# Two of the last four output blocks begun in side banks, the last 128 features in strips of their own, stores shared by two queues, and a new instruction order in an attention kernel on one core

## The chip, the cores and the metric

The kernel runs on one core of a Trainium2 chip. The metric is the device time of one execution in microseconds. The core has five engines, each with an instruction stream of its own that is executed in order: TensorE (PE in the profile, with its weight loads as PEld), VectorE (DVE), ScalarE (ACT), GpSimd (POOL) and SyncE (SP, which here only issues DMAs). Engines wait for each other with semaphores. Matmuls write to PSUM, which has eight banks of 128 partitions by 512 float32 values; everything else lies in SBUF or, for copies that change the layout, in DRAM scratch tensors.

## The reference

Two attention layers read their own inputs' weights but the same activations x (2048 tokens, 640 features, 32 heads of 20), and a gate mixes their outputs:

```python
x = A_x
g = _sigmoid((x * gate_w).sum(-1, keepdims=True))
a = _A_ref(x, A_wqkv, A_wo)      # full softmax attention: scores of 2048 x 2048 for each of 32 heads
b = _B_ref(x, B_wqkv, B_wo)      # each token looks at 8 tokens, at distances 0, 2, ... 14 behind it
return g * a + (1 - g) * b
```

In `_A_ref`, `scores = q k^T * Dh ** -0.5`, `p = softmax(scores)`, `o = p v`, and `o @ wo`. `_B_ref` does the same over the 8 gathered keys. The output is 2048 x 640 in bfloat16. Nearly all of the work is the exponential of 32 x 2048 x 2048 scores.

## The kernel before, in words

**Groups and tiles.** The 2048 queries are taken in four chunks of 512 (`qc`), the 32 heads in eight sets of four (`q`). A pair (qc, q) is a group, 32 in all, in the order of `GROUPS`. A group has 64 units: 16 blocks of 128 keys times 4 heads. One unit is a score matmul of 32 rows (20 features, a bound that keeps the exponent in range, and zeros) by 512 queries; four heads lie in four row strips of the array and run side by side. `next_tile` (line 1890) forms a score tile of two or three units, `qk` (1942; the matmuls are line 1955) writes it to one of two PSUM tensors, `score0` and `score1`, and `exp` (1970; line 1973) turns it into `ebuf` on ScalarE, 1024 or 1536 columns at a time. `pv` (1982; line 2018) multiplies `ebuf` by the values into `obank`, two tiles later. `vA` holds a column of ones, so that the denominators come out with the sums.

**Rides.** ScalarE can't take all units. A fourth kind of unit "rides" with a tile of two: its scores go to the third bank of the tile's PSUM tensor, and VectorE makes a coarse exponential of it by rounding to the bits of a bfloat16 (`clamp`, line 1932, into `uD`); three shifted copies (`gen_d`, line 1048, or on POOL `piece`, line 1079, into `eD`) with weighted values (`gen_vs`, line 1098) correct it, so such a unit needs four PV matmuls instead of one. `wanted` (1813) decides whether a tile takes a ride, `lone` (2052) sends one by itself.

**Banks.** PSUM holds `score0` and `score1` (three banks each), `obank` and `side0`. All other matmuls (projections, local attention, output blocks) borrow one of three side banks: bank 0 is `side0`, banks 1 and 2 are the third banks of `score0` and `score1`, and `bank()` (655) hands out whichever is free first. So a third unit, a ride and a side matmul compete for the banks 1 and 2.

**Who sets the order.** The order of every engine is computed while the program is built. `_Sched.task` (263) appends an instruction to its engine's list and keeps an estimate of when it ends; side work is written as Python generators (`gen_...`) with priorities, which `run_side` and `spend` step forward while the estimate shows room before the next score tile. Twenty-two knobs of that (slacks, due times, thresholds, how many products POOL takes, when a filler matmul is put in to keep TensorE busy, line 2039) come from the table `PLAN` (52), which has an entry for every fifth or tenth tile. Changing one entry changes the order of everything behind it.

**Side work.** `gen_q1`, `gen_qd`, `gen_kd` and `gen_v` project queries, keys and values; `gen_bproj` and `gen_b` do the local attention in eight pieces of 256 tokens (`u`): products on VectorE (line 1216) and POOL, sums over features by TensorE (1229), an exponential `eT` on ScalarE (1261), a trip through DRAM (`scr_e`, then `eB`) that spreads it over partitions (`gen_relay`, 1177), products with the values (1325) and sums (1337). `gen_norm` (972) normalises a finished group and moves it by DMA to `oTd`, and `gen_fold` (1488) forms the output rows of the first three chunks, 128 rows at a time, from `oB` (local) and `oTd` (full).

**The end.** The last four output blocks (the 512 queries of the last chunk) can't wait for `gen_fold`. `gen_prefold` (1386) sums, for their columns 0 to 511 of blocks 0 and 1 and for the last 128 columns of all four, what is ready early, and parks it in SBUF (`pre`). `gen_prefold2` (1425) sums columns 0 to 511 of the blocks 2 and 3 in a side bank each and leaves them there (`tail_bank`). It begins when the normalised heads of all groups but the last are there and no more rides are to come (`d_over`). `tail` (1436) then adds on TensorE (line 1447) what came late: two feature chunks for the last 128 columns of all four blocks, which lie side by side in one bank of `score1` (the strips), the same two chunks for columns 0 to 511 of blocks 0 and 1 in two banks of `score0` (the halves), and finally the last group's heads (`oN`, from `gen_norm_last`, 936) for strips, side banks and halves. VectorE adds strips (1471) and halves (1480) to what was parked, ScalarE copies the blocks 2 and 3 out (1477), and four DMAs of 128 rows store them (1485): blocks 2 and 3 from ScalarE's queue, 0 and 1 from SP's.

## Time and profile before

| what | us |
|---|---|
| median of 3 runs (778.37 to 778.88) | 778.65 |
| profiled execution, its own time | 778.55 |
| span from its first to its last instruction | 776.7 |
| ScalarE busy, of which line 1973 | 756.5, 742.9 |
| TensorE busy | 749.7 |
| VectorE busy | 697.6 |
| POOL busy | 359.0 |
| mean of one exponential of 1024 columns (513 of them) | 1.076 |
| mean of one exponential of 1536 columns (196 of them) | 1.520 |

The profile gives one execution. A line of it names an engine, the line of the kernel, the operation, the tile written and the tiles read, the count, and then the busy time with the mean of one, and the idle time of the engine before it with what ended that idle time. Consecutive instructions of an engine overlap a little, so a mean is longer than the step from one to the next. The timeline gives start and length in us from the start of the span, with equal neighbours merged (the form shown is the first one's). A granted clock of 9 in the page's row of tenths means the full TensorE clock.

### The profile page before, as it was taken

The numbers are of one execution on the slowest core, as the hardware profiler recorded it, in microseconds if no ns is written. First come the engines' busy times: TensorE is split into PE (matmuls) and PEld (weight loads), VectorE is DVE, ScalarE is ACT, GpSimd is POOL, SyncE is SP. The second block draws the span as 40 slices with busy tenths as digits, with TensorE's granted clock in tenths as the row PEclk, the third lists the DMA queues.
The fourth block names the chain that finished last, engine by engine and source line by source line (L and its number), as shares of the span: only waits on it lengthen the run. The fifth ranks groups of instructions, "written<-read, shape, count | busy, mean of one in ns | idle before, by whom it ended". The sixth has DMA issues, their size and how long they took to land.

```text
span 776.7 us, 30340 instructions
## 1 busy us (share of the span) xinstructions
PE 749.7 (97%) x12484; PEld 290.9 (37%) x12484; DVE 697.6 (90%) x1270; ACT 756.5 (97%) x751; POOL 359.0 (46%) x616
## 2 busy tenths in 40 slices
PE   9999999999999999999999999999999999999997
PEld 6433333232334333334344334433444433343232
DVE  6798989999899999979899989999999998899895
ACT  6999999999999999999999999999999999999995
POOL 4345744455453542545355445434545433344441
PEclk9999999999999999999999999999999999999999
DMA  7421221021121435201124112323124133102301
GB/s 231 117 60 39 48 66 40 21 47 35 34 72 47 100 79 115 61 26 37 38 64 110 32 48 67 96 66 92 45 51 106 34 78 96 52 19 63 88 12 36
DMA packets 71457, 49.91 MB, mean 64 GB/s; under 512 B 43096, under 2 KB 64872, under 8 KB 71320
## 3 DMA queue, kind: packets, MB, share of 16 engines
q1 hardware_dynamic: 70376, 47.54, 24.4%
q8 instruction: 100, 1.64, 0.9%
q10 hardware_dynamic: 944, 0.43, 0.2%
q14 instruction: 37, 0.30, 0.1%
HBM read 32.79 MB, written 7.62 MB: 52 GB/s over the span
## 4 chain that ended last, share of the span: by engine, by line
PE 49%; ACT 30%; issue 13%; DVE 6%; DMA 1%; SPq 0%; ACTq 0%; DVEq 0%
ACT ebuf L1973 30%; PE score L1955 16%; PE obank L2018 14%; PE side L681 12%; PE score L681 4%; DVE uD L1932 2%; DVE eD L1048 1%; DMA oB<-in_A_x_dram 1%; PE side L1337 1%; PE side L1229 1%; PE score L2039 1%; DVE kvw L1216 0%; PE score L1666 0%; PE obank L2039 0%; DVE dst L831 0%
## 5 line engine op out<-in xcount | busy, mean ns | idle before, releaser
L1973 ACT ACTIVATE ebuf<-score 128x1024 bf16<-128x1024 f32 (+1 forms) x710 | 742.9, 1198 | 5.1 <-PE score L1955 3.6
L1932 DVE TENSOR_SCALAR uD<-score 128x512 int16<-128x512 f32 x433 | 291.3, 684 | 33.8 <-PE score L1955 31.6
L1955 PE MATMUL score<-qT,kT 32*128 32x512 bf16 x1856 | 258.8, 384 | 12.6 <-ACT ebuf L1973 9.3
L1079 POOL TENSOR_TENSOR eD<-uD,two 128x256 int32<-128x256 int32 x331 | 198.2, 613 | 136.0 <-DVE eD L1048 61.6
L1048 DVE TENSOR_SCALAR eD<-uD 128x2048 int16<-128x2048 int16 (+3 forms) x302 | 173.2, 596 | 3.1 <-PE obank L2018 2.3
L2018 PE MATMUL obank<-ebuf,vA 128*21 128x512 bf16 x1615 | 152.8, 385 | 1.3 <-ACT ebuf L1973 1.1
L1955 PEld LDWEIGHTS score<-qT,kT 32*128 32x128 bf16 x1856 | 63.8, 91 | 209.0 <-ACT ebuf L1973 148.1
L1098 POOL TENSOR_TENSOR vS<-vA,vw 128x252 bf16<-128x252 bf16 x109 | 67.2, 617 | 110.3 <-DVE eD L1048 64.5
L2018 PE MATMUL obank<-eD,vS 128*21 128x512 bf16 x1299 | 113.1, 379 | 0.0
L681 PE MATMUL side<-xT,wBs 128*32 128x256 bf16 x2400 | 97.7, 282 | 1.7 <-DVE qkvB L1154 0.8
L681 PEld LDWEIGHTS side<-xT,wBs 128*32 128x32 bf16 x2400 | 67.4, 142 | 34.1 <-issue 16.8
L1021 POOL TENSOR_TENSOR oN<-oTt,oN 128x256 bf16<-128x256 f32 x60 | 45.2, 754 | 50.8 <-DVE eD L1048 27.8
L2018 PEld LDWEIGHTS obank<-ebuf,vA 128*21 128x21 bf16 x1615 | 37.0, 89 | 82.9 <-issue 56.7
L1325 DVE TENSOR_TENSOR kvw<-kvw,eB 128x2048 bf16<-128x2048 bf16 (+1 forms) x40 | 45.8, 1171 | 0.0
L1154 DVE CAST qkvB<-side 128x512 bf16<-128x512 f32 (+1 forms) x72 | 42.1, 594 | 2.5 <-PE side L681 2.4
L1216 DVE TENSOR_TENSOR kvw<-qkvB 128x2048 bf16<-128x2048 bf16 (+2 forms) x40 | 43.6, 1124 | 0.1
L2018 PE MATMUL obank<-uD,vA 128*21 128x512 bf16 x433 | 42.3, 379 | 0.0
L2018 PEld LDWEIGHTS obank<-eD,vS 128*21 128x21 bf16 x1299 | 31.8, 91 | 20.0 <-issue 2.5
L1006 POOL TENSOR_TENSOR rcp<-rcp,gA 128x16 f32<-128x16 f32 x30 | 7.4, 248 | 58.1 <-DVE eD L1048 33.2
L1955 PE MATMUL score<-woBp,kT 32*128 32x512 bf16 x192 | 29.5, 384 | 1.8 <-ACT ebuf L1973 1.8
L681 PE MATMUL side<-xT,kvw 128*32 128x512 bf16 (+1 forms) x360 | 29.8, 382 | 0.3 <-DVE vA L907 0.2
L1207 POOL TENSOR_TENSOR kvw<-qkvB 128x256 bf16<-128x256 bf16 x29 | 17.5, 614 | 26.9 <-DVE kvw L1216 11.4
(201 smaller groups left out, 578.9 us busy)
## 6 DMA issues: line engine op xcount, KB each, us to landing
kvw<-scr_v SPq DMA_DIRECT2D x32, 336.5 KB
oN<-scr_n SPq DMA_DIRECT2D x60, 128.0 KB
scr_v<-qkvB SPq DMA_DIRECT2D x32, 85.0 KB
wBs<-in_B_wqkv_dram SPq DMA_DIRECT2D x5, 480.0 KB
WqP<-in_A_wqkv_dram SPq DMA_DIRECT2D x14, 160.0 KB
oTd<-oN SPq DMA_DIRECT2D x108, 20.0 KB
out_dram<-outsb SPq DMA_DIRECT2D x12, 160.0 KB
qT<-dst SPq DMA_DIRECT2D x93, 20.0 KB
```

Source lines behind the costliest of these rows:

```text
L681: ins = e.matmul(o[j:k, :], l(j) if callable(l) else l[:, j:k], r, start=(first and i == 0), stop=(last and i == n - 1), skip_group_check= ...
L1021: T("pool", 0.73, lambda e, cols=cols: e.tensor_tensor(oN[0][:, cols], oTt[:, cols], rcpR[:, cols], ALU.mult), reads=["oTt", "oN%d" % i], ...
L1048: T("dve", 0.065 + 0.1334 * (n - m), lambda e, k=k, sl=sl, m=m: e.tensor_scalar(eD[:, sl % NS, 512 * m:512 * n].bitcast(I16), uD[d % 2][:, ...
L1079: T("pool", PDUR, lambda e: e.tensor_tensor(eD[:, sl % NS, 512 * i:512 * (i + 1)].bitcast(I32), uD[d % 2][:, 512 * i:512 * (i + 1)].bitcas ...
L1098: T("pool", 0.607, lambda e: e.tensor_tensor(vS[:, d % 2, :, :], _ap(vA, (kb * NQ + q) * 4 * DV, [[0, K - 1], [1, 4 * DV]]), _ap(vw, 0, [[ ...
L1154: t = TB(dvc(n * TOK), lambda e, o=o, i=i: e.tensor_copy(o, i), reads=[("side", b)], writes=[key])
L1216: TB(dvc(n_ * TOK, 2), lambda e: e.tensor_tensor(o, i0, i1, ALU.mult), reads=["qB", "kB"], writes=prods(i, range(n_)) + olds(), port=True)
L1325: TB(dvc(n_ * 2 * TOK, 2), lambda e: e.tensor_tensor(o, i0, i1, ALU.mult), reads=rd, writes=prods(i, range(2 * n_)), port=True)
L1932: t = T("dve", 0.598, lambda e: e.tensor_scalar(uD[d % 2][:, 512 * i:512 * (i + 1)].bitcast(I16), side[x], UOFF, 0.0, op0=ALU.add, op1=ALU ...
L1955: ins = e.matmul(o, kT[32 * j:32 * j + 32, q, kb * P:(kb + 1) * P], qT[qbuf[g]][32 * j:32 * j + 32, :], start=True, stop=True)
L1973: exps[s] = T("act", actc(512 * n), lambda e: e.activation(ebuf[s % NE][:, 0:512 * n], score[s % 2][:, 0:512 * n], ACTF.Exp, scale=LN2 / S ...
L2018: ins = e.matmul(obank[32 * j:32 * j + DV, :], v, src, start=(kb == 0), stop=(last and k >= len(lst) - 4), skip_group_check=True)
```

## The change

It has five parts. They are told here in the order in which they act.

1. `PLAN` has other values from the first tile on and 128 entries instead of 121, so the instruction order differs on every engine from about the tenth tile to the end. The computation is the same.
2. Rides in another bank: where the knob `FRT` is 0 or more (ten of the table's entries), a tile that carries a ride may take a third unit too, and the ride's scores go to bank 0 or to the other tile's third bank (`rbank`).
3. Two of the last blocks in side banks: `gen_prefold2` asks for bank 0 for block 2 and bank 1 for block 3, begins block 2 when the last group has begun, with the local part and the first three feature chunks, and takes the other two chunks when the heads of all groups but the last are there. While 14 units or fewer of the last group are left, tiles leave bank 1 free (`TLAST` in `crowded`).
4. The last 128 columns: the strips of the blocks 2 and 3 lie in one bank of `score1` and those of 0 and 1 in the next, each pair with a key of its own, and VectorE adds each pair by itself; the halves have keys of their own as well. `gen_norm_last` turns the first half of the heads back before it scales the second, and the last group's matmuls run in the order block 2, strips 2 and 3, block 3, strips 0 and 1, half 0, half 1.
5. Stores: blocks 2 and 0 go by SP's queue, 3 and 1 by ScalarE's; the planner's estimate of a store has a case of its own (`svc < 0`), which changes no instruction by itself.

```diff
 PLAN = {
-    0: ((0.326, 0.478), 0.0, 1, 1.0, 0.79, -1.09, -0.25, 10.72, 2.0, 9.17, 0.45, 0.36, 3.46, 3.61, 0.0, 0.59, 1, -2.32, 0.3, -1.0, (2, 2), 0.2),
+    0: ((0.326, 0.478), 0.0, 1, 1.0, 0.79, -1.09, -0.25, 5.46, 2.0, 9.17, 0.45, 0.36, 3.46, 3.61, 0.0, 0.59, 1, -2.32, 0.3, -1.0, (2, 2), 0.2),
...
-        for op, h in ((turn_o, 1), (turn_o, 0), (inv, 1), (inv, 0), (gate_r, 1), (gate_r, 0), (scale_o, 1), (scale_o, 0), (back, 1), (back, 0)):
+        for op, h in ((turn_o, 1), (turn_o, 0), (inv, 1), (inv, 0), (gate_r, 1), (gate_r, 0), (scale_o, 1), (back, 1), (scale_o, 0), (back, 0)):
             op(h)
...
     def gen_prefold2():
-        while not (done.get("prefold1") and d_over() and all(done.get(("norm", POS[QCN - 1, q])) for q in range(1, NQ)) and done.get("wz")):
-            yield ("cond",)
-        rd = [("oTd", (QCN - 1) % 2, q) for q in range(NQ)] + ["woA_d"] + WOB + WQ + oBk(QCN - 1, range(2))
+        early = sorted({h // 4 for f in range(FE) for h, o, r, m in pieces[f]})
+        while not (done.get("prefold1") and cur["g"] >= NG - 1 and done.get("wz")):
+            yield ("cond",)
+        rd = [("oTd", (QCN - 1) % 2, q) for q in early] + ["woA_d"] + WOB + oBk(QCN - 1, range(2))
         qs = None
         for blk in (2, 3):
-            b = yield from bank()
-            yield from mm_group(b, fold_mms(side[b][:, :], blk, qs, 0, 512, True), rd, mmc(512), last=False)
+            while blk > 2 and not d_over():
+                yield ("cond",)
+            b = yield from bank(blk - 2)
+            yield from mm_group(b, fold_mms(side[b][:, :], blk, qs, 0, 512, True, range(FE)), rd, mmc(512), last=False)
+            while not all(done.get(("norm", POS[QCN - 1, q])) for q in range(1, NQ)):
+                yield ("cond",)
+            yield from mm_group(b, fold_mms(side[b][:, :], blk, qs, 0, 512, True, range(FE, CN)),
+                                [("oTd", (QCN - 1) % 2, q) for q in range(NQ)] + WQ, mmc(512), first=False, last=False)
             tail_bank[blk] = b
...
-        strip = lambda blk: b3[:, blk * P:(blk + 1) * P]
+        sof = lambda blk: 512 * (blk < 2) + blk % 2 * P
+        strip = lambda blk: b3[:, sof(blk):sof(blk) + P]
...
-        mm(("score", 1), [m_ for blk in range(4) for m_ in first(strip(blk), blk, q, 512, D)], False, rl)
-        mm(("score", 0), [m_ for blk in range(2) for m_ in first(half(blk), blk, q, 0, 512)], False, rl)
+        for h in (1, 0):
+            mm(("strip", h), [m_ for blk in (2 * h, 2 * h + 1) for m_ in first(strip(blk), blk, q, 512, D)], False, rl, [("score", 1)][:h])
+        for blk in range(2):
+            mm(("half", blk), first(half(blk), blk, q, 0, 512), False, rl, [("score", 0)][blk:])
         run_until(("norm", NG - 1))
+        for h, blk in ((1, 2), (1, None), (1, 3), (0, None), (0, 0), (0, 1)):
+            if blk is None:
+                mm(("strip", h), [fold_mms(strip(i), i, q, 512, D, False)[0] for i in (2 * h, 2 * h + 1)], True, rd[h])
+            elif h:
+                mm(("side", tail_bank[blk]), fold_mms(side[tail_bank[blk]][:, :], blk, q, 0, 512, False), True, rd[h])
+            else:
+                mm(("half", blk), fold_mms(half(blk), blk, q, 0, 512, False), True, rd[h])
         for h in (1, 0):
-            mm(("score", 1), [fold_mms(strip(blk), blk, q, 512, D, False)[0] for blk in (2 * h, 2 * h + 1)], True, rd[h])
...
-        T("dve", dvc(512), lambda e: e.tensor_tensor(
-            _ap(stage, 3 * 1024 + 512, [[D, 4], [1, P]]), _ap(b3, 0, [[P, 4], [1, P]]),
+            T("dve", dvc(256), lambda e, h=h: e.tensor_tensor(
+                _ap(stage, 3 * 1024 + 512 + 2 * h * D, [[D, 2], [1, P]]), _ap(b3, sof(2 * h), [[P, 2], [1, P]]),
...
-            T("act" if blk > 1 else "sp", 2.0, lambda e, blk=blk, row=row: e.dma_start(out_v[row:row + P, :], tout[blk]),
-              reads=[("tout", blk), "tout_r"], writes=[("out", row)], dma=True, iss=0.45)
+            T("act" if blk % 2 else "sp", 2.0, lambda e, blk=blk, row=row: e.dma_start(out_v[row:row + P, :], tout[blk]),
+              reads=[("tout", blk), ("tout_r", blk // 2)], writes=[("out", row)], dma=True, iss=0.45, svc=-0.6)
...
                 if ride:
-                    break
+                    alt = [b for b in ((0, 3 - x) if FRT >= 0.5 else (0,) if FRT >= 0 else ()) if not bank_used[b] and bank_free[b] <= now + 0.05]
+                    if not alt or sum(bank_used) == NB - 1 or lo == 4 * ahead[g][1]:
+                        alt = None
+                        break
...
+    TLAST = 14
+
     def crowded(x):
...
-        return sum(bank_used) == 1 and any(ent[3][0] == "bank" and ent[0] <= xprio() for ent in gens) and bank_free[x] <= min(
+        return cur["g"] == NG - 1 and x == 1 and 4 * ahead[NG - 1][1] - ahead[NG - 1][0] <= TLAST and "prefold" not in done or sum(bank_used) == 1 and any(ent[3][0] == "bank" and ent[0] <= xprio() for ent in gens) and bank_free[x] <= min(
             [bank_free[b] for b in range(NB) if not bank_used[b]])
...
-                    add_gen(gen_prefold2(), 2.3)
+                    add_gen(gen_prefold2(), 0.9)
```

More of the change, by code (lines that the diff above doesn't have):

```diff
@@ L309, in task @@
             t.end = start + dur
-            if stream == "sp" and start > 35.0:
+            if svc < 0:
+                self.ring = max(self.ring, start + 0.55) - svc
+                t.end = self.ring + 1.0
+            elif stream == "sp" and start > 35.0:
                 fin = max(max(self.ring, start + 1.4) + svc, start + 1.4 + iss * (nd - 1) + svc / nd)
@@ L653, in _build, with bank @@
     xheld = [None]
-    def bank():
+    def bank(*only):
         while True:
-            got = yield ("bank",)
+            got = yield ("bank", *only)
             if got is not None:
@@ L1450, in mm @@
             T("pe", sum(0.215 if o.shape[-1] > 128 else 0.06 for o, _, _ in lst), fn, reads=rd, mode="col",
-              **({"accum": [key]} if accum else {"writes": [key]}))
+              **({"accum": [key]} if accum else {"writes": [key] + list(old)}))
         b3 = score[1]
@@ L1795, in _build @@
     rides = []
+    rbank = []
     UNIT = 0.46
@@ L1964, in qk @@
         t = T("pe", 0.2155 * max(js.count(j) for j in js), fn, reads=sorted(rd, key=str),
-              writes=[("score", s % 2)] + ([("side", x)] if len(lst) == 3 else []), mode="row")
+              writes=[("score", s % 2)] + ([("side", x)] if len(lst) >= 3 else []) + ([("side", rbank[s])] if rides[s] and rbank[s] != x else []),
+              mode="row")
         if rides[s]:
-            clamp(t, d, i, x)
+            clamp(t, d, i, rbank[s])
     def exp(s):
```

23 lines of the change are left out of this document (9 added, 14 removed), and 241 rows, old and new, of the table PLAN.

## The prediction

> **What bounds the kernel now.** I read the page first (busy time by engine, then its costliest groups), then ScalarE's part of the timeline, then the timeline of the last 12 us, then the chain that ended last.
>
> ```profile
> PE 749.7 (97%) x12484; PEld 290.9 (37%) x12484; DVE 697.6 (90%) x1270; ACT 756.5 (97%) x751; POOL 359.0 (46%) x616
> ...
> PEclk9999999999999999999999999999999999999999
> ...
> L1973 ACT ACTIVATE ebuf<-score 128x1024 bf16<-128x1024 f32 (+1 forms) x710 | 742.9, 1198 | 5.1 <-PE score L1955 3.6
> ```
>
> ScalarE spends 742.9 us of a span of 776.7 in one line, the exponentials of the score tiles. By form these are 513 of 1024 columns, 196 of 1536 and one of 512. Its timeline gives the pace at which they follow each other when nothing holds them:
>
> ```profile
> 16.30 0.47 ACT L1693 ACTIVATE kT<-obank,onesrow 128x256 bf16<-128x256 f32 x1
> 17.29 33.27 ACT L1973 ACTIVATE ebuf<-score 128x1536 bf16<-128x1536 f32 x31 [0.53 <-PE score L1955]
> ...
> 50.77 6.50 ACT L1973 ACTIVATE ebuf<-score 128x1024 bf16<-128x1024 f32 x7
> ...
> 253.62 1.08 ACT L1973 ACTIVATE ebuf<-score 128x1024 bf16<-128x1024 f32 x1
> ...
> 580.53 2.92 ACT L1973 ACTIVATE ebuf<-score 128x1536 bf16<-128x1536 f32 x2
> ...
> 583.19 2.95 ACT L1973 ACTIVATE ebuf<-score 128x1536 bf16<-128x1536 f32 x2
> ...
> 765.85 1.69 ACT L1973 ACTIVATE ebuf<-score 128x1024 bf16<-128x1024 f32 x2
> ```
>
> Seven of 1024 columns take 6.50 us and one lasts 1.08, so the step is (6.50-1.08)/6 = 0.904 us. Two of 1536 lie between 580.53 and 583.19: 1.33 us a step. The exponentials start at 17.29 and the last ends at 765.85+1.69 = 767.54, 750.25 us later. At the free pace they need 513x0.904 + 196x1.331 + 0.73 = 725.4; the 21 other ScalarE instructions in between add about 5.6 (0.47, 0.11 and 0.14 from their neighbours' starts). So 19.2 us are lost because a score tile came late, in pieces of mostly under half a microsecond that the page's 5.1 us of idle shows only in part. From the starts of all tiles, stretches of 50 tiles lose between 1.1 and 2.6 us, 1.8 in the mean (the other instructions, 0.4, included).
>
> The remaining 9.15 us (767.54 to 776.7) are the end:
>
> ```profile
> 767.59 0.61 PE L2018 MATMUL obank<-ebuf,vA 128*21 128x512 bf16 x8 [0.28 <-ACT ebuf L1973]
> 768.03 0.82 PE L681 MATMUL score<-woBp,oB 128*32 128x512 bf16 x12
> ...
> 768.26 0.78 DVE L940 STREAM_TRANSPOSE oTt<-obank 128x256 f32<-128x256 f32 x2 [3.43 <-PE obank L2018]
> ...
> 769.39 0.78 DVE L955 TENSOR_TENSOR oN<-oTt,rcp 128x256 bf16<-128x256 f32 x2
> ...
> 770.06 0.50 DVE L959 STREAM_TRANSPOSE oN<-oN 128x128 f32<-128x128 f32 x2
> ...
> 770.85 0.39 PE L1447 MATMUL score<-WqP,oTd 128*32 128x512 bf16 x4
> 771.07 0.28 PE L1447 MATMUL score<-outsb,oN 128*32 128x128 bf16 x8
> ...
> 771.95 0.69 DVE L1471 TENSOR_TENSOR kvw<-score,kvw 128x512 bf16<-128x512 f32 x1 [1.39 <-PE score L1447]
> ...
> 773.15 0.68 DVE L1480 TENSOR_TENSOR kvw<-score,qabs 128x512 bf16<-128x512 f32 x1
> ...
> 773.26 0.94 SPq L1485 DMA_DIRECT2D out_dram<-kvw  x2
> ```
>
> The reader is to see that the normalised heads oN stand ready at 770.56, but TensorE comes to them only at 771.07: it is still clearing output-block work that stands ahead in its queue. The chain of work that ended last says the same:
>
> ```profile
> 767.59 0.61 PE obank L2018 x8
> 768.20 1.73 PE score L681 x32
> 769.93 1.42 PE score L1447 x56
> ...
> 771.95 0.69 DVE kvw L1471
> 772.64 0.60 DVEq L357
> ```
>
> **The sum's base.** The profiled execution took 778.55 us, of which 776.70 are the span; the median of the runs is 778.65, 0.10 above it. A measurement of this kernel can tell about 0.2% (1.56 us) from no change.
>
> **Head: 0.** The list of head operations is untouched; the first tile still leaves at 17.29.
>
> **Exponentials: +0.2.** Counted in the built program, the new order has 500 of 1024, 205 of 1536 and one of 512 (1616 units of 512 columns instead of 1615, one clamp on VectorE fewer): 452.0 + 272.9 + 0.7 = 725.6 against 725.4. ScalarE remains the bound. The Trainium skill, in "ScalarE: Activation LUTs" under "Rules for kernel authors", budgets about 0.3 us for each ACTIVATE plus 0.83 ns an element; by that, 13 short ones fewer and 9 long ones more would be an estimated -0.8, and the sum 1.0 lower than mine. The trace disagrees: the fixed part in 0.904 us for 1024 columns is about 0.05 us.
>
> **Tiles that come late: -1.4.** The planner's table is new for nearly every stretch, so every stretch between the first ten tiles and the end is ordered anew. What does not change: PV, projection and local-attention matmuls differ by three instructions; VectorE's shifted copies become fewer and longer (178 of 2048 columns for 169, 19 of 512 for 36), with row means of 704 and 297 ns and the other forms -0.4 us in all; POOL makes 20 copies fewer (0.61 us each, on an engine busy 46%). SP's queue holds as many transfers of each kind as before (60 reads of oN, 16 eB loads and so on), in another order. Two things ease TensorE, whose lateness is the loss. There are 706 score tiles instead of 710, and a tile costs 0.32 us (753.86 to 754.18 in the timeline) and about 0.10 of switching beside its neighbours: 4x0.42 = -1.7. And of the places where a PV matmul waits for VectorE, POOL or ScalarE there are 309 instead of 351; the page's waits put 10.8, 6.6 and 1.3 us on such places, and 12% of these 18.7 is -2.2. The 72 missing filler matmuls (304 for 376, 18 groups of four at 0.215 us = 3.9 us) count for nothing, since they stand where TensorE had nothing to do. TensorE's 3.9 us only help where it was late. Bounds: -3.9 and 0. But some 38 tiles of 710 carry 10.8 of the 19.2, and which of them are touched is not to be seen, so I stay nearer to 0 and take -1.4. A new order is also a new draw: the 14 stretches scatter by 0.43 us, which is 1.6 over all, so 8 times in 10 within 2.1 either way. The rides in another bank change little by themselves: 4 of 432 go to the spare bank.
>
> **End: -0.9.** Removed from behind the last PV matmul: 16 of the 32 matmuls of block 3 (4 groups, 0.86 us), which now stand ahead of it. Ahead there is room: before, 8 matmuls ran from 766.70 to 767.13 and TensorE then waited until 767.59, so 8 more (0.43) end as the last exponential does, and the other 8 stand one and two tiles earlier. TensorE's backlog then ends at 771.07-0.86 = 770.2. VectorE becomes the bound there: the first half's back transpose follows its own scaling, at about 769.9 instead of 770.06, ready at 770.2; the second half's is pushed behind scaling two and comes 0.3 later, at 770.9. First-half matmuls (0.54 us) run from about 770.35, second-half ones (0.54) from 771.0, and TensorE ends at 771.7 instead of 772.3. The strip addition becomes two of 256 columns, 0.42 each (the row of 256-column L955 is 0.44) and 0.34 apart, the first from 771.0 beside the matmuls. The two 0.60 steps of L1480 then end at 773.0 against 773.83. This adds one instruction, 0.1 us against one of 512. Stores: SP's second issue at 773.86 landed by 775.91; now ScalarE issues blocks 3 and 1, SP 2 and 0, the last at 773.0; ScalarE has nothing else left, and its issues took 0.35 and 0.45 us and landed 1.84 and 1.93 us later. Gain between 0.6 (TensorE's end alone) and 1.2 (0.86 and the second issue's 0.34); I take 0.9, by the additions' ends. One wait moves closer: block 2's last 8 matmuls need the oTd moves of the last group but one, and the last two score tiles stand behind them. The transpose ahead of the moves stands about 16 us before the last exponential's end, the moves need 3.69 to issue and some 1.9 to land, the use comes 2.5 before the end: 8 us of cover, so 0. The bank kept free during the last 14 units changes forms only, and is in the count above.
>
> **Sum.** 778.55 + 0.2 - 1.4 - 0.9 = 776.45, rounded 776.5.
>
> **Rivals.**
> *Only the end gains:* the new order loses as the old (19.2), as the near-equal tally of TensorE's work per pair of tiles suggests (326 pairs over ScalarE's pace before, 318 after). 777.9, inside 0.2%.
> *The new order is much better:* every stretch loses what the better half of them did before, 1.4 instead of 1.8: 14x0.35 = -4.9, and 773.0. For it speaks only that TensorE's order is lighter in 8 of 14 stretches.
> *The new order loses more:* in tiles 300 to 350, 450 to 500 and 600 to 650 TensorE's work exceeds ScalarE's by 1.2, 0.1 and 0.3 us, where it stayed 0.5, 1.0 and 0.2 below. TensorE is in order, so each excess is ScalarE's idle time. Five of 14 stretches at the worst row (2.6 us for 1.8) make +3.9 where I have -1.4: 781.8. It decides from 3.7 us above my sum on. Against it: over all tiles that work is 5.9 us lighter.
> *The last local-attention piece is late:* its exponential eT now stands 12 tiles ahead of the first matmul that sums its products, where 23 tiles lay between (5x1.33 + 8x0.904 + 0.6 = 14.5 us to the next need). Issue, two DMA trips and product take 0.84+1.80+1.9+1.18+1.9+1.2+0.6 = 9.4 by the rows, so 5 us of cover. Were 19.8 us needed from eT to the first product as before (713.95 to 733.74), TensorE would stand for 7: 783.5. Against it: VectorE did not wait for that product, the old order merely put it there.
> *The clock:* the granted clock is 1.00 everywhere except 0.97 in the last 9.1 us, where TensorE empties. If each of the 18 missing filler groups left such a dip (0.27 us), this costs 4.9: 781.4. The Trainium skill, "TensorE: Matmul & The Clock Gate", Part 1, says that an idle window of some 3.4 us halves the clock. Against it: the emptiest 25 us still have TensorE busy for 23.1.
>
> **How the numbers follow.** Forecast 0.54 (0.50 of it beyond 0.2%), much better 0.10, only the end 0.22, loses more 0.08, late piece 0.04, clock 0.02. Faster 0.60, same 0.26, slower 0.14. Range 774.0 to 779.4: it leaves out the second case for the most part and the three slow ones; the likeliest case alone spans 774.4 to 778.6 (2.1 either way).
>
> **What would show it.** ScalarE's last exponential should end near 766.3 with 706 instructions and a busy time within 2 us of 742.9. Behind it the oN matmuls of block 2 should begin about 770.35-767.54 = 2.8 us after it (3.5 before), the last L1480 successor should end 5.4 us after it (6.3), the span 8.2 (9.15). The step on which I trust least is the lateness: should the exponentials end at 767.5 or later, it failed; should VectorE's second back transpose or a store come later than said, the end did.

## The result and the profile after

The changed kernel takes 776.25 us (median of 6, 775.56 to 776.46), the kernel before in the same series 778.72 (778.37 to 779.77): a ratio of 0.9965, 95% interval 0.9953 to 0.9978. The forecast was 776.5. From the page of the changed kernel, busy times and the line of the exponentials:

```profile
PE 743.5 (96%) x12409; PEld 291.0 (38%) x12409; DVE 696.8 (90%) x1263; ACT 756.6 (98%) x747; POOL 353.8 (46%) x603
...
PEclk9999999999999999999999999999999999999999
...
L2000 ACT ACTIVATE ebuf<-score 128x1024 bf16<-128x1024 f32 (+1 forms) x706 | 743.2, 1198 | 3.0 <-PE score L1981 1.6
```

Line numbers have moved: the exponentials stand in line 2000 (1973 before), score matmuls in 1981, PV in 2045, fillers in 2066, side matmuls in 691, the tail's in 1464, strip additions in 1490, half additions in 1499, stores in 1504. By the rows of the two traces the orders first differ at 58.5 us, at the 40th tile (not from about the tenth, as the section on the change has it). ScalarE is the bound as before: 706 exponentials, 743.2 us for 742.9. Its timeline has the start of the first and the end of the last:

```profile
18.00 27.84 ACT L2000 ACTIVATE ebuf<-score 128x1536 bf16<-128x1536 f32 x26 [0.53 <-PE score L1981]
...
765.80 0.60 ACT L2000 ACTIVATE ebuf<-score 128x512 bf16<-128x512 f32 x1
```

With the prediction's pace (0.904 and 1.331 us a step) the span of one profiled execution falls into four terms. "Loss" is the time from the first exponential's start to the last one's end, less that pace; the other ScalarE instructions (about 5.6) are in it for both kernels.

| term, us | before | after | difference | predicted |
|---|---|---|---|---|
| first exponential begins | 17.29 | 18.00 | +0.71 | 0 |
| exponentials at their own pace | 725.36 | 725.59 | +0.23 | +0.2 |
| loss | 24.89 | 22.82 | -2.07 | -1.4 |
| behind the last exponential | 9.21 | 8.02 | -1.19 | -0.9 |
| span | 776.75 | 774.43 | -2.32 | -2.1 |

The timeline of the end, all engines:

```profile
766.47 0.61 PE L2045 MATMUL obank<-ebuf,vA 128*21 128x512 bf16 x8
766.90 0.82 PE L691 MATMUL score<-woA_d,oTd 128*32 128x512 bf16 x12
767.13 0.78 DVE L950 STREAM_TRANSPOSE oTt<-obank 128x256 f32<-128x256 f32 x2 [6.78 <-PE obank L2045]
...
768.75 0.31 DVE L969 STREAM_TRANSPOSE oN<-oN 128x128 f32<-128x128 f32 x1
...
769.12 0.10 PEld L1464 LDWEIGHTS side<-outsb,oN 128*32 128x32 bf16 x4 [0.37 <-DVE oN L969]
769.12 0.40 PE L1464 MATMUL side<-outsb,oN 128*32 128x512 bf16 x4
769.34 1.18 PE L1464 MATMUL score<-outsb,oN 128*32 128x128 bf16 x28
769.43 0.31 DVE L969 STREAM_TRANSPOSE oN<-oN 128x128 f32<-128x128 f32 x1
...
769.68 0.89 DVE L1490 TENSOR_TENSOR kvw<-score,kvw 128x256 bf16<-128x256 f32 x2
769.80 0.23 PEld L1464 LDWEIGHTS score<-outsb,oN 128*32 128x32 bf16 x16 [0.29 <-DVE oN L969]
...
770.19 1.37 SPq L1504 DMA_DIRECT2D out_dram<-kvw  x2
770.49 0.68 DVE L1499 TENSOR_TENSOR kvw<-score,dst 128x512 bf16<-128x512 f32 x1
770.68 1.45 ACTq L1504 DMA_DIRECT2D out_dram<-kvw  x2
771.08 0.68 DVE L1499 TENSOR_TENSOR kvw<-score,qabs 128x512 bf16<-128x512 f32 x1
```

The last exponential ends at 766.40. The matmuls of the last heads begin at 769.12, 2.7 us later (2.8 forecast, 3.5 before), as soon as the first half of the heads stands ready (769.06); the last addition ends at 771.76, 5.35 us later (5.4 forecast, 6.3 before). TensorE's weight loads (PEld) now wait for VectorE's back transposes, 0.37 us for the first half of the heads and 0.29 for the second, where the kernel before had the heads ready 0.5 us before TensorE came to them. So VectorE sets the pace there, as the prediction said. The chain that ended last shows this only in part, since TensorE still has matmuls to run up to that point:

```profile
767.07 0.86 PE score L691 x16
767.94 1.31 PE score L1464 x48
769.25 0.27 PE side L1464 x4
769.52 0.60 PE score L1464 x20
...
770.57 0.60 DVE kvw L1499
```

### The profile page after: what moved, and what is told of

Read it like the earlier page. It is cut to its first block, busy times and chain, and to the rows that moved or that the text cites. A ratio compares the mean times of both kernels' runs of the same rounds, so it can differ in the third digit from the quotient of the medians.

```text
span 774.4 us, 30166 instructions
## 1 busy us (share of the span) xinstructions
PE 743.5 (96%) x12409; PEld 291.0 (38%) x12409; DVE 696.8 (90%) x1263; ACT 756.6 (98%) x747; POOL 353.8 (46%) x603
## 4 chain that ended last, share of the span: by engine, by line
PE 45%; ACT 33%; issue 15%; DVE 6%; DMA 1%; SPq 0%; ACTq 0%; DVEq 0%
ACT ebuf L2000 33%; PE score L1981 14%; PE obank L2045 13%; PE side L691 11%; PE score L691 4%; DVE uD L1958 2%; DVE eD L1058 1%; DMA oB<-in_A_x_dram 1%; PE side L1239 1%; PE score L2066 0%; PE score L1685 0%; PE side L1347 0%; PE obank L2066 0%; DVE dst L841 0%; DVE kvw L1226 0%
## 5 line engine op out<-in xcount | busy, mean ns | idle before, releaser
L2000 ACT ACTIVATE ebuf<-score 128x1024 bf16<-128x1024 f32 (+1 forms) x706 | 743.2, 1198 | 3.0 <-PE score L1981 1.6
L1958 DVE TENSOR_SCALAR uD<-score 128x512 int16<-128x512 f32 x428 | 286.0, 681 | 30.0 <-PE score L1981 28.0
L1089 POOL TENSOR_TENSOR eD<-uD,two 128x256 int32<-128x256 int32 x311 | 186.7, 615 | 123.3 <-DVE eD L1058 59.3
L1108 POOL TENSOR_TENSOR vS<-vA,vw 128x252 bf16<-128x252 bf16 x108 | 65.4, 606 | 111.7 <-DVE eD L1058 66.0
L2045 PE MATMUL obank<-eD,vS 128*21 128x512 bf16 x1296 | 110.7, 379 | 0.0
L691 PE MATMUL side<-xT,wBs 128*32 128x256 bf16 x2400 | 95.6, 281 | 0.7 <-DVE rQ L1301 0.5
L1031 POOL TENSOR_TENSOR oN<-oTt,oN 128x256 bf16<-128x256 f32 x60 | 47.5, 791 | 58.7 <-DVE eD L1058 29.3
L1226 DVE TENSOR_TENSOR kvw<-qkvB 128x1792 bf16<-128x1792 bf16 (+2 forms) x40 | 44.4, 1133 | 0.1
L691 PE MATMUL side<-kvw,xT 128*32 128x160 bf16 (+1 forms) x760 | 28.5, 262 | 0.5
```

The lines of the kernel that those rows point to most:

```text
L691: ins = e.matmul(o[j:k, :], l(j) if callable(l) else l[:, j:k], r, start=(first and i == 0), stop=(last and i == n - 1), skip_group_check= ...
L1031: T("pool", 0.73, lambda e, cols=cols: e.tensor_tensor(oN[0][:, cols], oTt[:, cols], rcpR[:, cols], ALU.mult), reads=["oTt", "oN%d" % i], ...
L1089: T("pool", PDUR, lambda e: e.tensor_tensor(eD[:, sl % NS, 512 * i:512 * (i + 1)].bitcast(I32), uD[d % 2][:, 512 * i:512 * (i + 1)].bitcas ...
L1108: T("pool", 0.607, lambda e: e.tensor_tensor(vS[:, d % 2, :, :], _ap(vA, (kb * NQ + q) * 4 * DV, [[0, K - 1], [1, 4 * DV]]), _ap(vw, 0, [[ ...
L1226: TB(dvc(n_ * TOK, 2), lambda e: e.tensor_tensor(o, i0, i1, ALU.mult), reads=["qB", "kB"], writes=prods(i, range(n_)) + olds(), port=True)
L1958: t = T("dve", 0.598, lambda e: e.tensor_scalar(uD[d % 2][:, 512 * i:512 * (i + 1)].bitcast(I16), side[x], UOFF, 0.0, op0=ALU.add, op1=ALU ...
```

## The experiments

Each kernel ran beside the kernel before on one chip. The table gives medians, the kernel before in the same series, the ratio's 95% interval, and from one profiled execution the terms of the table above; "additions" is the end of the last addition, counted from the end of the last exponential.

| kernel | median | before | ratio | first | loss | additions | span - last exponential |
|---|---|---|---|---|---|---|---|
| before | 778.72 | | | 17.29 | 24.89 | 6.29 | 9.21 |
| changed | 776.25 | 778.72 | 0.9953-0.9978 | 18.00 | 22.82 | 5.35 | 8.02 |
| old table | 776.68 | 778.81 | 0.9966-0.9983 | 18.27 | 25.53 | 5.35 | 7.67 |
| old end | 778.00 | 778.81 | 0.9982-0.9999 | 17.07 | 22.64 | 6.51 | 9.80 |
| small fillers | 776.80 | 778.81 | 0.9971-0.9988 | 17.93 | 23.80 | 5.35 | 8.14 |
| score matmuls doubled | 789.48 | 778.81 | 1.0120-1.0156 | 18.10 | 37.55 | 5.35 | 7.99 |
| old back order | 776.61 | 778.86 | 0.9956-0.9980 | 17.49 | 22.98 | 5.40 | 8.40 |
| old queues | 776.68 | 778.86 | 0.9956-0.9981 | 17.25 | 22.64 | 5.35 | 8.19 |
| PV cut | 777.01 | 778.86 | 0.9966-0.9984 | 17.50 | 21.87 | 5.34 | 8.21 |
| entry 400 nudged | 798.18 | 778.86 | 1.0229-1.0257 | 17.92 | 36.78 | 13.76 | 16.07 |
| PV doubled | 785.65 | 778.66 | 1.0075-1.0106 | 17.49 | 32.25 | 5.35 | 8.05 |
| eleven local nudges | 776.11 | 778.66 | 0.9955-0.9978 | 17.80 | 22.70 | 5.35 | 7.97 |
| old table, entry 485 nudged | 803.91 | 778.66 | 1.0308-1.0336 | 17.73 | 31.17 | 24.56 | 27.34 |
| one strip addition | 776.96 | 778.35 | 0.9971-0.9990 | 17.84 | 22.85 | 5.63 | 8.63 |

Two columns say how to read the rest. Kernels with the same order lose the same: the changed kernel, old back order, old queues, eleven nudges and one addition lie between 22.64 and 22.98, and the additions end at 5.35 wherever the end's code is the same. What scatters from execution to execution is the start, 17.07 to 18.27 in instructions that no kernel changed, and the landing of the last stores. The profiled execution need not be a typical one: those of "PV cut" and "old queues" are the shortest of their kernels (774.97 and 775.48 us).

**The table and the end, each alone.** The old table in the changed code, and the old end in the changed order:

```diff
-PLAN = { (128 entries) }
+PLAN = { (the 121 entries of the kernel before) }
```

> The changed kernel with the old table: the instruction order is that of the kernel before on every engine up to TensorE's 12159th of 12458 matmuls, and only the end is new. Theory (the parts add up, the order of the stretches brought most of it): the exponentials lose what they lost before, 24.9 us with the other ScalarE instructions, and end near 767.4 (17.3 + 725.1 + 24.9), the end behind them takes 8.0 to 8.2 instead of 9.2, so 777.4 to 777.7, 1.0 to 1.2 below the kernel before. Rival (the end's gain hangs on the new order, TensorE's queue being emptier there): the end takes 9.0 or more and the time is 778.4 or more. Second rival (the end brings all of it): 776.5 or less.

```diff
-    def gen_prefold2(): ... block 2 in bank 0, block 3 in bank 1, begun early
-    def tail(): ... strips by pairs, stores in turn
-    def gen_norm_last(g): ... scale 1, back 1, scale 0, back 0
+    (the three functions of the kernel before)
...
-    add_gen(gen_prefold2(), 0.9)
+    add_gen(gen_prefold2(), 2.3)
...
-        return cur["g"] == NG - 1 and x == 1 and 4 * ahead[NG - 1][1] - ahead[NG - 1][0] <= TLAST and "prefold" not in done or sum(...
+        return sum(...
```

> The changed kernel with the old end: the new table and the rides in another bank, but blocks 2 and 3 begun late, one strip bank, old order of the last matmuls and old stores; the order is that of the changed kernel up to TensorE's 12215th of 12411 matmuls. Theory (the parts add up): exponentials 497 x 0.904 + 207 x 1.331 + 0.7 = 725.5, loss as in the changed kernel 22.8, ended near 766.4, the end behind them 9.2 as before: 777.3 to 777.7, 1.0 to 1.4 above the changed kernel. Rival (the changed kernel's smaller loss was a matter of that one execution): 778.5. Rival (the end's gain is in the order): 776.3.

In the traces the parts add up. The old table keeps the old loss (25.53; 0.5 of the 0.64 above 24.89 arose ahead of the 700th tile, where its order is that of the kernel before) and has the new end, 5.35 for 6.29. The old end keeps the new loss (22.64) and pays 6.51. So the end's code is worth 0.94 us of engine time in the old order and 1.16 in the new, and the new order about 2.1 of loss. The medians put it otherwise, -2.1 for the end and -0.8 for the order; their intervals are -1.3 to -2.6 and -0.1 to -1.4. Both kernels missed what was expected of them: 776.68 where 777.4 to 777.7 was expected and 776.5 stood for "the end brings all of it", 778.00 where 777.3 to 777.7 was expected. And both profiled executions stand at an edge: that of the old table is the longest of its eleven (778.38) and has the latest start of all traces, that of the old end is the shortest of its eleven (776.94) and has the earliest. With such starts the medians do not settle the split, and the old end's kernel, by its trace 1.85 below the kernel before (2.07 in the exponentials' stage, less 0.22 at the end), lies outside the interval of its own runs; why stays open. What is firm is the sum, and that each part brings some of it.

**Parts of the end.** Three kernels undo one thing each:

```diff
-        for op, h in (..., (scale_o, 1), (back, 1), (scale_o, 0), (back, 0)):
+        for op, h in (..., (scale_o, 1), (scale_o, 0), (back, 1), (back, 0)):
```

> The changed kernel with one thing undone: the first half of the last heads is turned back only after the second is scaled. The first matmul of the last heads then waits for it: ready about 0.3 us later than in the changed kernel (769.7 for 769.4), the second half's about as early as there. Theory: TensorE's last work, the additions and the stores come 0.1 to 0.4 us later, counted from the end of the last exponential 8.1 to 8.4 us instead of 8.0, the time 0.2 us longer. Rival (the second half decides alone): no change. Everything before the end loses what the changed kernel loses, 22.8 us, as its order is the same.

```diff
-            T("act" if blk % 2 else "sp", 2.0, lambda e, blk=blk, row=row: e.dma_start(...
+            T("act" if blk > 1 else "sp", 2.0, lambda e, blk=blk, row=row: e.dma_start(...
```

> The changed kernel with the old store queues: blocks 2 and 3 from ScalarE, 0 and 1 from SyncE. Theory of the prediction's upper bound: SyncE's second issue has to wait for its first, 0.34 us more. Rival: the additions of the halves are 0.6 us apart and an issue takes 0.36, so the last store is issued when its data are ready from either queue, 0 us; the end takes 8.0 us either way.

```diff
-        for h in (1, 0):
-            T("dve", dvc(256), lambda e, h=h: e.tensor_tensor( ... strips of one pair ...
+        T("dve", dvc(512), lambda e: e.tensor_tensor( ... strips of all four ...
```

> The changed kernel with one thing undone: the strips of all four blocks added by one VectorE instruction of 512 columns instead of two of 256 (the two pairs of strips change places in PSUM for that). Counted from the end of the last exponential the changed kernel's additions end at 5.35 us. Theory (the two additions run beside the last matmuls, the first ready 0.34 earlier): the single one starts when the second pair of strips is done, about 3.6 after the last exponential, takes 0.60, and the additions end at 5.4 to 5.5. Rival of the prediction's bounds (two instructions cost 0.1 more and the last matmuls set the end anyway): 5.25. Everything before the end as in the changed kernel.

The order of the back transposes is worth 0.05 us (5.40 for 5.35): the last heads' matmuls begin 0.18 later, but the second half sets the end. Two strip additions instead of one are worth 0.28, more than the 0.05 to 0.15 expected. VectorE's timeline with one addition has it waiting 0.41 us before it, since it needs the last pair of strips as well:

```profile
770.01 0.69 DVE L1489 TENSOR_TENSOR kvw<-score,kvw 128x512 bf16<-128x512 f32 x1 [0.41 <-PE score L1464]
770.62 0.68 DVE L1498 TENSOR_TENSOR kvw<-score,dst 128x512 bf16<-128x512 f32 x1
```

If the parts add up, that leaves 0.94 - 0.05 - 0.28 = 0.61 for what was not undone alone: blocks 2 and 3 begun ahead of the last PV matmul, and the last matmuls in another order; the rides in another bank were not tried alone either. The queues move the additions by nothing. From the last addition to the end of the span there are 2.3 to 3.0 us in nine executions with the new queues (2.7 in the mean) and 2.84, 2.92 and 3.29 in three with the old: 0.3 may be there, but the ranges overlap.

**Does TensorE's amount of work decide the loss?** Three kernels keep the changed kernel's order and change only how long some matmuls are:

```diff
-            for g, kb, j, o in lst:
+            for g, kb, j, o in (lst[:1] if s % 8 == 4 and s > 15 else []) + lst:
                 q = GROUPS[g][1]
                 ins = e.matmul(o, kT...
```

> The changed kernel, its order unchanged, but in one score tile of eight the first score matmul is issued twice (86 more, same product): 86 x 0.215 = 18.5 us more for TensorE, spread evenly. Theory (a share of TensorE's work decides lateness; the prediction made 1.4 of 3.9 us, 0.36): 6.7 us longer, between 4 and 10. Rival (the loss does not come from the amount of TensorE's work, and the new order gained by where things stand): less than 2 us longer. Rival (TensorE is the bound of every stretch): 16 us or more.

```diff
+            w = 32 if units and tile_of[units[0]][0] % 16 == 4 and not last and all(v_[1] for v_ in lst) else 512
             for k, (g, kb, j, v, src) in enumerate(lst):
-                ins = e.matmul(obank[32 * j:32 * j + DV, :], v, src,
+                ins = e.matmul(obank[32 * j:32 * j + DV, 0:w], v, src[:, 0:w],
```

> The changed kernel, its order unchanged, with the PV matmuls that begin in one score tile of sixteen cut from 512 query columns to 32 (204 matmuls, 51 groups of four, about 51 x 0.18 = 9 us of TensorE; those products are left out of the output). Theory (a share of TensorE's work decides lateness; doubling matmuls made 0.6 of the added time): 3 to 5.5 us shorter, as long as the granted clock stays full. Rival (what is late is late for other reasons, only added work hurts): less than 1 us shorter. Rival (the clock, as where the fillers were cut): granted clock under full in single places, time 1 to 2 us longer there.

```diff
+            twice = units and tile_of[units[0]][0] % 16 == 4 and not last and all(v_[1] for v_ in lst)
-            for k, (g, kb, j, v, src) in enumerate(lst):
+            for k, (g, kb, j, v, src) in enumerate(lst + lst if twice else lst):
```

> The counterpart of the kernel with fewer PV columns: in the same places, the PV matmuls that begin in one score tile of sixteen are issued twice (204 more, 51 groups of four, 51 x 0.215 = 11 us; the output counts these products double), order otherwise unchanged. Taking 9 us away there gave 0.95. Theory (TensorE's order is packed so that the slack ahead of the score tiles is used up: work added costs, work taken away gives little): 4 to 8 us longer, near 0.6 of what is added, as with the doubled score matmuls. Rival (PV is not on the score tiles' path and its price is the same both ways): 1 to 1.5 us longer.

PV doubled adds 11 us to TensorE and 9.43 to the loss (32.25 - 22.82), 0.86 of it and more than the 4 to 8 expected. PV cut in the same places takes away 9 us by the count of matmuls (7.4 by TensorE's busy time, 743.5 to 736.1) and gives 0.95, about a tenth. The doubled score matmuls add 18.5; two of the four executions took 787.9, 11.6 more than the changed kernel (0.63), the other two 791.0. The profile of one of these has a stretch that the doubling alone does not explain: TensorE waited for a weight matrix from DRAM, and the granted clock fell behind that wait:

```profile
326.48 0.61 PE L691 MATMUL score<-woBp,oB 128*32 128x512 bf16 x8 [1.96 <-DMA woBp<-in_B_wo_dram]
...
326.00:330.00 4.00, 3.52 (x41) 1.04 (x45) 2.04 (x4) 1.60 (x2) 0.22 (x1) 0.69 0.14 31
```

(The second row gives the busy time of PE, PEld, DVE, ACT and POOL in that stretch, then the granted clock, 0.69.) So the expected 0.36 both ways was wrong: added work costs 0.6 to 0.9 of itself, relief brings next to nothing. One place, at the 25th tile, shows how. TensorE's timeline in the changed kernel:

```profile
43.19 0.61 PE L2045 MATMUL obank<-ebuf,vA 128*21 128x512 bf16 x8
43.63 0.82 PE L2045 MATMUL obank<-eD,vS 128*21 128x512 bf16 x12
44.38 0.39 PE L1981 MATMUL score<-qT,kT 32*128 32x512 bf16 x3
```

The same place with PV doubled (the second copies), and ScalarE behind it:

```profile
43.76 0.61 PE L2046 MATMUL obank<-ebuf,vA 128*21 128x512 bf16 x8
44.19 0.82 PE L2046 MATMUL obank<-eD,vS 128*21 128x512 bf16 x12
44.95 0.39 PE L1981 MATMUL score<-qT,kT 32*128 32x512 bf16 x3
...
45.38 1.02 ACT L2000 ACTIVATE ebuf<-score 128x1024 bf16<-128x1024 f32 x1 [1.13 <-PE score L1981]
```

TensorE there with PV cut to 32 columns:

```profile
42.75 0.24 PE L2046 MATMUL obank<-eD,vS 128*21 128x32 bf16 x12
43.40 0.39 PE L1981 MATMUL score<-qT,kT 32*128 32x512 bf16 x3 [0.42 <-ACT ebuf L2000]
...
44.32 0.39 PE L1981 MATMUL score<-qT,kT 32*128 32x512 bf16 x3 [0.20 <-ACT ebuf L2000]
```

The five PV groups fill the time between two score tiles. Doubled, the next exponential waits 1.13 us. Cut, the score matmul waits 0.42 us for ScalarE to release its PSUM tensor, and all but 0.22 of the relief is thrown away: the exponential behind it starts 26.60 us after the first one, where the changed kernel has 26.82. Six tiles on, nothing is left of the 0.22 either. There is no stock of finished score tiles that time gained here could be put into.

**Is a new order a draw?** The prediction took 1.6 us of scatter for it. Three kernels nudge the first knob of a few entries of the table:

```diff
-    400: ((0.34, 0.55), 0.4, 1, 1.0, ...
+    400: ((0.371, 0.581), 0.4, 1, 1.0, ...
```

> The changed kernel with one of its table's entries nudged (first knob of entry 400, 0.34 and 0.55 to 0.371 and 0.581): the order differs on all engines from about the 430th tile on. The work is the same to the matmul, 502 exponentials of 1024 columns and 204 of 1536 (725.4 instead of 725.6 us), but for 96 more filler matmuls. Theory of the prediction (a new order is a new draw, 1.6 us over all stretches, so 1.0 over the six it touches; equal work, equal loss on average): 776.3 within 1.3, the loss of tiles 450 to 700 10.5 within 1.3. Rival (the table's values were fitted to their own order, any other order loses more): over 1.5 us longer.

```diff
-    105, 195, 325, 365, 375, 620: ((a, b), ...
+    105, 195, 325, 365, 375, 620: ((a + 0.031, b + 0.031), ...
-    70, 80, 160, 225, 295: ((a, b), ...
+    70, 80, 160, 225, 295: ((a - 0.031, b - 0.031), ...
```

> The changed kernel with the first knob of eleven entries of its table moved by 0.031 (up at 105, 195, 325, 365, 375, 620; down at 70, 80, 160, 225, 295), chosen because the order then differs only for a few tiles behind each and falls back into the old one; counts of exponentials, matmuls and copies are the same but for 8 fillers. Theory (the table was fitted, each place stands near its best): of the eleven places most lose more or the same, the sum over them is 0.5 to 3 us more loss. Rival (the order in detail does not matter, only the amounts): sum within 0.3 us either way.

```diff
-    485: ((0.34, 0.51), 0.41, 1, ...
+    485: ((0.371, 0.541), 0.41, 1, ...
```

> The kernel before with one entry nudged in the same way (entry 485, 0.34 and 0.51 to 0.371 and 0.541): a new order from about the 520th tile on, 517 x 0.904 + 194 x 1.331 = 725.6 us of exponentials instead of 725.4, 93 more matmuls, nearly all fillers. Theory (both tables were fitted to their own orders, so the step from one to the other is not a draw): over 5 us longer than the kernel before. Rival (only the new table is so brittle): within 1.5 us of it.

Small local differences are worth nothing either way (22.70 for 22.82; each place moved by 0.2 us or less), so the expectation that each place stands near its best failed. A nudge that does not fall back into the old order costs 22 us in the new table and 25 in the old, for the same work but for fillers and a few forms of exponentials. Of this 14.0 and 6.3 are loss, 8.1 and 18.1 stand at the end. Between the tiles 400 and 700 the kernel with entry 400 nudged loses 24.2 where the changed one loses 10.6, and its end takes 16.1 us, of which TensorE's timeline gives the reason:

```profile
783.97 1.78 PE L691 MATMUL side<-woBp,oB 128*32 128x512 bf16 x20 [2.55 <-DVE kvw L1413]
785.53 1.93 PE L691 MATMUL side<-woA_d,oTd 128*32 128x512 bf16 x16
...
787.66 1.41 PE L691 MATMUL score<-woBp,oB 128*32 128x512 bf16 x20
```

Blocks 2 and 3, which the changed kernel begins ahead of the last exponential, begin here 3.9 us behind the end of it (780.03): they wait for a copy of parked sums (line 1413), which VectorE comes to only behind the last heads. In the old table's nudged kernel five products of the local attention are still to be done behind the last exponential. So in both the side work is not finished in time. The granted clock falls in these ends as well (0.57 from 784 to 788, and 0.50 from 780 to 790 in the other kernel), which makes them longer. That later entries are set for a state that is not there any more, so that a table and its order are one fitted whole, fits all three kernels, but two nudges do not show it in general. In these two cases, at least, another order of the same work was no random redraw about the same mean.

**The fillers and the clock.** All fillers cut to 32 columns:

```diff
-                ins = e.matmul(o[32 * j:32 * j + 32, :], w..., xT[:, 0, 1536:2048], ...
+                ins = e.matmul(o[32 * j:32 * j + 32, 0:32], w..., xT[:, 0, 1536:1568], ...
```

> The changed kernel, its order unchanged on all engines, with its 304 filler matmuls cut from 512 columns to 32; nobody reads their product, the output is the same. That takes some 76 groups x (0.215 - 0.04) = 13 us from TensorE. Theory (fillers stand where TensorE has nothing to do, and 72 fewer of them cost and brought nothing): time within 0.4 us of the changed kernel, granted clock full. Rival (the clock): the granted clock dips in the emptier slices and the time rises by over 1 us. Rival (fillers delay score tiles): the time falls by over 1 us, up to 13 x 0.36 = 4.7.

The executions spread from 776.28 to 778.40 us, seven of the twelve at 776.3 to 776.9 with a mean granted clock of 0.997 to 1.0, the three longest (777.9 to 778.4) at 0.993 to 0.995. Five lie within the 0.4 us that were expected; the full clock that was expected did not hold. In the profiled one the order loses 0.5 less up to tile 600 and 1.5 more behind it. The reason stands in its windows (read as above), with one row of TensorE's timeline:

```profile
730.00:733.00 3.00, 2.65 (x45) 0.86 (x42) 3.00 (x6) 3.00 (x4) 1.59 (x3) 1.00 0.75 143
733.00:735.00 2.00, 1.03 (x10) 0.31 (x14) 1.05 (x2) 2.00 (x3) 0.00 (x0) 0.94 0.08 21
735.00:737.00 2.00, 2.00 (x40) 0.88 (x32) 0.00 (x0) 2.00 (x2) 0.00 (x0) 0.50 0.18 38
...
734.36 0.39 PE L1981 MATMUL score<-qT,kT 32*128 32x512 bf16 x3 [0.95 <-ACT ebuf L2000]
```

The same stretch of the changed kernel, where the same wait of 0.95 us stands:

```profile
733.00:735.00 2.00, 1.08 (x15) 0.21 (x9) 2.00 (x3) 2.00 (x3) 0.85 (x1) 1.00 0.15 34
735.00:737.00 2.00, 1.97 (x51) 1.10 (x51) 0.34 (x2) 2.00 (x3) 0.00 (x0) 1.00 0.10 26
...
735.03 0.39 PE L1981 MATMUL score<-qT,kT 32*128 32x512 bf16 x3 [0.95 <-ACT ebuf L2000]
```

With short fillers ahead of that wait the clock falls to 0.50 for 3.4 us, and the next exponential is 1.1 us late; a second dip, from 748.5 to 751.7, costs 0.4 twice. The kernel with cut PV matmuls was profiled only in an execution at full clock, but its runs point the same way: two executions at a mean clock of 1.0 took 774.97 and 775.12, the other nine, at 0.994 to 0.998, took 776.7 to 778.4.

## Why the prediction was right, and where it was not

**Exponentials, +0.2: right.** 706 instructions, +0.23 by the steps. The busy time rose by 0.3; by the estimate from the Trainium skill's budget ("ScalarE: Activation LUTs", "Rules for kernel authors") it would have fallen by 0.8. That budget is given for a bias as a pointer operand, which the call in line 1973 does not pass.

**Head, 0: right of the change, not of the execution.** The +0.71 is the start's scatter: the same instructions began the first exponential anywhere from 17.07 to 18.27.

**Lateness, -1.4: size right, reason wrong.** The loss fell by 2.07 in the traces (by the median of the old end's kernel the order brings 0.8), inside the bounds. But the step that "TensorE's 3.9 us only help where it was late", of which 1.4 were taken, does not carry it: relief in the order as it stands was worth 0.10 of itself in the one kernel that gave it, which makes 0.4 of the 3.9. And "a new order is also a new draw" holds for the scatter alone: stretch by stretch the new order differs from the old by 0.68 us (the standard deviation of 14 differences), about what two draws at 0.43 would give, but the two nudged orders lost 14.0 and 6.3 us more, so a draw need not scatter about the loss of the order that it replaces. That the size came out is luck in part. What remains is where things stand. Up to tile 600 the new order loses 18.6 for 21.9, and from 600 to 700 it loses 4.2 for 2.8. An example with a loss in the old order, TensorE and ScalarE in the kernel before:

```profile
124.91 0.39 PE L1955 MATMUL score<-woBp,kT 32*128 32x512 bf16 x3 [0.34 <-ACT ebuf L1973]
...
126.31 0.83 PE L681 MATMUL side<-xT,WqP 128*32 128x512 bf16 x12
126.97 0.39 PE L2018 MATMUL obank<-ebuf,vA 128*21 128x512 bf16 x4
127.19 0.39 PE L2018 MATMUL obank<-uD,vA 128*21 128x512 bf16 x4
127.51 0.61 PE L1955 MATMUL score<-woBp,kT 32*128 32x512 bf16 x6
...
127.95 2.37 ACT L1973 ACTIVATE ebuf<-score 128x1024 bf16<-128x1024 f32 x2 [0.34 <-PE score L1955]
```

TensorE stands 0.34 us for ScalarE, has 1.2 us of other work between two score tiles right after, and ScalarE then waits 0.34. The changed kernel puts eight projection matmuls where that wait was, and ScalarE does not wait there. That the new table was fitted to such places is what the nudged kernels suggest; it was not shown tile by tile, and why the new order loses less stays open. The tally of VectorE's copies in that paragraph, -0.4 us in all, does not come out of the rows either: by their means the new counts cost 1.2 more, and the copies' busy time rose by 0.9, from 176.5 to 177.4; no term hangs on it.

**The rival "loses more": its reading was half right.** Tiles 300 to 350 lost 2.8 (1.9 before) and 600 to 650 2.6 (1.7), as the tally of TensorE's work against ScalarE's said; 450 to 500 stayed at 2.2. The other stretches made up for it: nine of the 14 lost less than before. "Much better" did not come true either, with 1.6 us a stretch where it had 1.4 and the kernel before had 1.8.

**The rival of the late local-attention piece: wrong.** From its exponential to the first product that needs it there are 12.3 us, where the prediction counted 14.5 and a need of 9.4, and VectorE, busy up to it, did not wait. ScalarE's, SyncE's and VectorE's timelines of the changed kernel:

```profile
734.66 0.81 ACT L1271 ACTIVATE eT<-side 128x512 bf16<-128x512 f32 x1
...
742.08 1.16 SPq L1196 DMA_DIRECT2D eB<-scr_e  x2
...
746.91 1.22 DVE L1335 TENSOR_TENSOR kvw<-kvw,eB 128x2048 bf16<-128x2048 bf16 x1
```

**The clock: wrong for this change, but near.** The granted clock stayed at 1.0 with 72 fillers fewer. That fillers "count for nothing" holds for time (0.5 us at most) and not for the clock.

**End, -0.9: right.** Engine time fell by 0.94 to the last addition, as forecast by that row. That VectorE becomes the bound there is right as well (the two waits of TensorE's weight loads above). Inside it the sizes differ: the new order of the back transposes made 0.05, since the second half of the heads decides; the split additions made 0.28, where the prediction had them cost 0.1; and the store queues' 0.34 was not seen. Against "only the end gains" speaks the loss of six kernels in the new order, all about 2 below the old, and the old end's median, whose interval just leaves out no gain.

**The sum.** 776.5 for a median of 776.25 is closer than its terms: in the two profiled executions the start came 0.71 later than forecast, loss and end 0.67 and 0.29 smaller, and these nearly cancel.

## What to carry to other kernels

Split the span into start, own pace of the bounding engine, loss and end, and compare term by term: here the loss of one order repeats within 0.7 us and the engines' end within 0.02, while the median carries a start that scatters by 1.2. Look where the profiled execution stands among the runs before its terms are taken for the kernel's. In an in-order engine that is packed between deadlines, added work cost 0.6 to 0.9 of itself here and relief brought a tenth; do not count relief until the trace shows a place where the gained time is taken up. An order written by a table of knobs has to be judged in the built order, stretch by stretch, since a nudge that changed next to no work cost 22 us.

## What the hardware showed beyond that

In identical order on five engines, with DMAs beside them, the exponentials of two executions start close to each other once the first has left: five kernels (one of them with the local nudges) stay within 0.3 us of the changed one over 740 us, and in the old order the largest distance is 0.73 (the kernel before against its nudged form, up to the 490th tile).

With small fillers the clock was halved for 3.4 us (734.8 to 738.2) although TensorE had no gap above 0.95 us. A gap of 0.95 us stands at full clock in the traces of the kernel before, the changed kernel, old back order, old queues and local nudges, so its length alone does not bring the drop. With small fillers TensorE was busy for 2.2 of the 3.5 us up to the drop by the records (731.5 to 735.0), and the changed kernel has 3.5 us with 2.4 (734.5 to 738.0) at the full clock, so the records' busy share hardly tells the two apart. Behind longer gaps the clock fell as well, each time for about 3.4 us: 1.96 us (score matmuls doubled) and 2.55 us (entry 400 nudged). The Trainium skill, "TensorE: Matmul & The Clock Gate", Part 1, speaks of an idle window of some 3.4 us. The length agrees with these dips; that the window must be idle does not.
